# Gated linear attention and a dropless mixture of experts: reordered scan step, work moved between ScalarE and VectorE

## Chip, cores and metric

The kernel runs on one core of one Trainium2 chip. Five engines work side by side, each through its own instructions in order: TensorE (PE, with its weight loads as PEld), VectorE (DVE), ScalarE (ACT), GpSimd (POOL) and SyncE (SP, which here mostly issues DMAs). The metric is the device time of one execution in microseconds (us), less being better. Before the change the median of three runs is 445.88 us (445.43 to 446.48).

## The reference

```python
# attention: B=4, H=8 heads, S=768, D=48
for t in range(S):
    state = alpha[:, :, t, :, None] * state + einsum('bhd,bhe->bhde', k[:, :, t], v[:, :, t])
    y[:, :, t] = einsum('bhd,bhde->bhe', q[:, :, t], state)
x = y.transpose(0, 2, 1, 3).reshape(N, 384)            # N = 3072 tokens
# experts: E=8, F=1024, each token goes to the one with the largest logit
logits = x @ w_gate
expert_idx = argmax(logits, axis=1)
gate_w = softmax(logits)[arange(N), expert_idx]        # 1e-9 added to the sum
for e in range(E):
    h = maximum(x[expert_idx == e] @ w1[e], 0.0)
    y[expert_idx == e] = h @ w2[e]
out = gate_w[:, None] * y
```

No token is dropped, so how many rows an expert gets is known only from the data.

## The kernel before

**The scan.** The sequence is cut into 6 chunks of 128 positions. A tile s = 4c + b is chunk c of batch b with all 8 heads, so there are 24 tiles (NT). Inside a chunk the recurrence is written as a masked product: with cp the running product of alpha and icp its inverse, `operands` makes k*icp and q*cp, `transposes` turns both (kT, qT), `scores` multiplies them per head pair into two PSUM banks sA and sB, `mask` makes dA and dB of them, and `attend` multiplies those with v. What earlier chunks leave comes through the state: `scale_state` scales it (U), `read_state` adds q times U, `keys_values` collects k times v in the same PSUM tile y, and `add_state` adds U and that to the new state (acc). `result` copies y to SBUF (yT), `rows` turns yT into token rows with the gate logits beside them, in PSUM bank x. `logits` adds the logits up (lgn) and takes their minimum (lmin; lgn holds the negated logits), `gate` takes the exponential (gex, its sum is gw), adds 1e-9 and takes the reciprocal, and `keep_rows` scales the rows by it (xs) and stores them in memory. Scaling the rows first is allowed because the gate weight is positive and the expert layers carry no bias.

`logs` takes the logarithm of alpha on ACT (lna), `cums` makes the running sums on PE (bank cum), then icp and cp on ACT, and then issues on ACT's queue one or two small DMAs (L405) that put a row of icp or cp into `dec`, for the decay between chunks: one in the first and in the last chunk with sums, two between. `decay_rows` multiplies these on POOL (er) and `decay_cols` transposes them (ep, then E on DVE), once in a chunk.

**Order.** The scan runs under a manual schedule: the text order of the loop (L656 to L712) is each engine's order. In step i the loop works on several tiles at once: scores, masks and attend of i, result and rows of i-1, logits, gate and keep_rows of i-2, transposes of i+1, operands of i+2, sums and logarithms of up to i+5 tiles. Loads of q, k, v and alpha go through SP two tiles at a time, sums run ahead until tile 23, so that steps from 19 on have none. `route` and the tables before it put the routing work (choice of expert, ranks, slots, one-hot matrices, token lists) into fixed steps. Bank x has one buffer: `rows` of one tile waits until `keep_rows` has read the tile before. At step 23 `early_turn` transposes 256 tokens of expert group 0 that are gathered while the scan still runs, and the tail (L715 to L742) mixes their first layer (`early_layer1`, 8 blocks) with the last rows, choices, ranks, counts and slots.

**The experts.** Group 0's other 168 rows run plainly: `gather` fetches token rows by indirect DMA on POOL, `turn` transposes them (tp on PE, xgT by a copy), `rest_layer1` does 8 blocks of three products with a relu from PSUM on ACT (L1052), `rest_layer2` the second layer. `places`, a Python generator, computes on DVE where each group begins and whether a group overflows; its last part (overflow counts xn, xi, xx) feeds a loop at the end that handles overflowing groups. Groups 1 to 7 run both layers in a Strassen-like form, whose sums of weights are made on DVE by `weight_sums` (s and th, L184 and L187); `layer1` takes a generator `beside` and advances it between its products, so that storing the last group's rows (`rows_out`) and for group 1 the weight sums of layer 2 are spread over it. `weights(i, layer)` reads the expert's number on SP and issues the load of its weights (1.5 MB).

Of the kernel before, what the change touches and what calls it, by code (L numbers as in the profile page):

```python
# [18 lines left out]
def kernel(  # L19
# [343 lines left out]
    with tc.tile_pool(name="ld", bufs=6) as ld, \  # L363
# [65 lines left out]
        def operands(s):  # L429
            d = st[s]  # L430
            kq = kqb[s % 3]
            for i, n, e in ((0, "k", "icp"), (1, "q", "cp")):
                nc.gpsimd.tensor_tensor(  # L433
                    by_half(kq[:, i]), d[n].rearrange("s (a p) d -> s a p d", a=2),
                    d[e][:].rearrange("s (a p d) -> s a p d", a=2, p=NP), op=ALU.mult,
                )

        def transposes(s):
            d = st[s]
            for i, n in enumerate(("kT", "qT")):  # L440
                tp = ps.tile([C, NP, C], F32, name="tp", bufs=2)
                for p in range(NP):
                    nc.tensor.transpose(tp[:, p, :], pair(kqb[s % 3][:, i], p), ident[:])  # L443
                d[n] = work.tile([C, NP, C], F32, name=n)

                if i and s < NT - B - 2:
                    nc.vector.tensor_copy(d[n][:], tp[:])  # L447
                else:
                    nc.scalar.copy(d[n][:], tp[:])
# [74 lines left out]
        def rows(s):  # L524
            d = st[s]
            d["x"] = ps.tile([C, NP, C], F32, name="x")
            for m in range(NP):
                for o in (0, HC):
                    nc.tensor.matmul(  # L529
                        d["x"][o : o + HC, m, : D2 + E], lhsT=d["yT"][:, m // 2, m % 2, o : o + HC], rhs=iw[:, m, :],  # L530
                        start=True, stop=True,
                    )
# [6 lines left out]
        def gate(s):  # L539
            d, t = st[s], s  # L540
            gex = work.tile([C, E], F32, name="gex")
            d["gw"] = work.tile([C, 1], F32, name="gw", bufs=4)
            nc.scalar.activation(gex[:], lgn[:, t, :], AF.Exp, bias=lmin[:, t : t + 1], scale=-1.0, accum_out=d["gw"][:])
            nc.vector.tensor_scalar_add(d["gw"][:], d["gw"][:], 1e-9)
            nc.vector.reciprocal(d["gw"][:], d["gw"][:])
# [91 lines left out]
        def tiles(t0, n):  # L637
# [6 lines left out]
            5 * B: [(one_hots, nc.vector, 11, 12)], 5 * B + 1: [(one_hots, nc.vector, 14, 15)], NT - 1: [(choose, 4)],  # L644
# [11 lines left out]
        for i in range(-4, NT):  # L656
            loads_for(i + 3)
            do(scores, i)
            if i == NT - 1:
                early_turn()  # L660
            do(result, i - 1)
            do(add_state, i - 1)
# [3 lines left out]
            do(mask, i, 1)  # L666
            if -2 < i < 0:
                idle(3)
            do(logits, i - 2)
            do(transposes, i + 1)  # L670
            sums = list(new_sums(i))

            if i < B:
                for s in sums[:1]:
                    cums(s)
            do(gate, i - 2)
            route(i)
            if i == NT - 2:
                si = next(se)[1]
                eg["si"] = lambda j, r: si[:r, j : j + 1]  # L680
            do(keep_rows, i - 2)
            if i >= B:
                for s in sums[:1]:
                    cums(s)
# [10 lines left out]
            do(attend, i)  # L695
            for s in sums[1:]:
                cums(s)
# [8 lines left out]
            for s in new_sums(i + 1):  # L706
                logs(s)
# [8 lines left out]
        result(last)  # L716
        logits(last - 1)
        early_layer1(0)
        rows(last)
        gate(last - 1)  # L720
        keep_rows(last - 1)
        early_layer1(1)
        logits(last)
        choose(NB - 1)
        ranks(NG - 1)
        gate(last)
        keep_rows(last)
        early_layer1(2)
        cps = ps.tile([C, NP, C], F32, name="sA").rearrange("p a c -> p (a c)")[:, : 2 * E]
        counts(NG - 1, cps)  # L730
# [30 lines left out]
    def turn(g):  # L761
        g["xT"] = wk.tile([C, DB, CAP0], F32, name="xgT")
        for j, r in blocks(g):
            tp = mps.tile([C, DB, C], F32, name="tp", tag="tp")
            for a in range(DB):
                nc.tensor.transpose(tp[:, a, :r], g["xg"][:r, j, a * C : (a + 1) * C], ident[:r, :r])  # L766
            nc.vector.tensor_copy(g["xT"][:, :, j * C : j * C + r], tp[:, :, :r])  # L767
# [208 lines left out]
    def places():  # L976
# [26 lines left out]
        nc.vector.tensor_mul(nb[:], nb[:], over[:])  # L1003
        ve = small2("ve")
# [14 lines left out]
        nc.vector.tensor_copy(xi[:], xx[0:1, 0, :])  # L1019

# [5 lines left out]
        yield xn, xi, xx  # L1026
# [14 lines left out]
    def rest_layer1(g):  # L1041
        n = g["n"]
        g["h"] = wk.tile([C, FB, CAP0], F32, name="h_sb")
        for f in range(FB):
# [7 lines left out]
            nc.scalar.activation(g["h"][:, f, :n], hp[:, :n], AF.Relu)  # L1052
# [28 lines left out]
    xn, xi, xx = next(pl)  # L1081
    def beside(i):

        yield from rows_out(groups[i - 1])
        if i == 1:
            for k_, _ in enumerate(weight_sums(groups[1], 2, nc.vector)):
                if k_ % 2:
                    yield

    for i, g in enumerate(groups):  # L1090
# [8 lines left out]
        if i:  # L1099
            layer1(g, beside(i), begin)  # L1100
        else:
            rest_layer1(g)
        weights(i + 2, 1)
        if i == 0:
            weights(1, 2)
        if i + 2 < E:
# [25 lines left out]

    nx = nc.values_load(xn[0:1, 0:1], min_val=0, max_val=NX)
# [47 lines left out]
```

## Time and profile before

| what | value |
| --- | --- |
| median of three runs | 445.88 us |
| the profiled execution, its own time | 446.82 us |
| its span, first to last instruction | 444.7 us |
| PE busy | 411.4 us (93%) |
| PEld busy | 349.2 us (79%) |
| DVE busy | 222.4 us (50%) |
| ACT busy | 170.3 us (38%) |
| POOL busy | 146.9 us (33%) |
| mean granted TensorE clock | 0.987 |
| first `scores` / last `rows` of the scan end | 10.7 / 160.4 us |

The profile is of one execution, 0.94 us above the median of the runs; 2.1 us of its time lie outside the span. Shares are means over the span: the scan (to about 160 us), the early tokens and group 0 (to about 200), and groups 1 to 7 are stages with limits of their own. In rows of the profile, "out<-in" gives the tiles by the program's names, "x" the count, and what stands behind the last bar or in brackets is how long the engine stood idle before the instruction and what ended that wait. ACTq is a DMA issue in ACT's queue. Where T is used, it is the start of a step's first `scores` product; for steps 0, 3, 13, 15, 18, 19 and 23 that is 10.71, 30.42, 92.30, 104.35, 122.47, 127.91 and 150.34 us.

### The profile page before, as it was taken

The page shows a single profiled execution, that of the slowest core. Times are in us where ns is not written, and L with a number is a line of the kernel's source. Part 1 is how long each engine was busy: PE and PEld are TensorE (multiplying, and loading weights), DVE is VectorE, ACT ScalarE, POOL GpSimd, SP SyncE. Part 2 cuts the span into 40 slices and gives each one's busy share as a digit, 9 for nine tenths or more (in the row PEclk, how much of TensorE's full clock was granted, in tenths as well). Part 3 has the DMA queues.
Part 4 walks back from the last instruction along what each step waited for, and adds up shares of the span by engine and source line. Part 5 has one row for each costly group of instructions (what it writes and reads, how often), then busy time and mean ns, then how long its engine had stood idle before and what let it go on. Part 6 is the DMA issues. An engine that isn't in the chain of part 4 may idle for free.

```text
span 444.7 us, 9321 instructions
## 1 busy us (share of the span) xinstructions
PE 411.4 (93%) x3566; PEld 349.2 (79%) x3566; DVE 222.4 (50%) x670; ACT 170.3 (38%) x452; POOL 146.9 (33%) x195
## 2 busy tenths in 40 slices
PE   7898999999998889889899999999999999999991
PEld 5567777877886676679769979979979979979970
DVE  3333645654566546622673474474474473583500
ACT  3565555555654331014412512512513513514411
POOL 3537444677568102700400240230240230201102
PEclk9999999999999999989999999999999999999996
DMA  9999999999540214458233252352353254100101
GB/s 175 202 196 221 214 206 195 241 236 208 124 110 29 68 55 165 124 180 291 60 141 118 79 201 87 110 197 73 124 196 102 94 193 147 46 2 18 33 0 51
DMA packets 119969, 59.07 MB, mean 133 GB/s; under 512 B 102806, under 2 KB 114159, under 8 KB 119924
## 3 DMA queue, kind: packets, MB, share of 16 engines
q1 hardware_dynamic: 114804, 48.80, 42.6%
q0 software_dynamic: 3424, 9.59, 6.3%
q8 instruction: 29, 0.48, 0.5%
q10 hardware_dynamic: 1696, 0.08, 0.2%
q14 instruction: 16, 0.13, 0.1%
HBM read 48.95 MB, written 9.58 MB: 132 GB/s over the span
## 4 chain that ended last, share of the span: by engine, by line
PE 54%; issue 5%; DVE 2%; ACT 1%; POOL 1%; POOLq 0%
PE pA L848 10%; PE pB L848 8%; PE pC L919 7%; PE pA L904 7%; PE pC L848 4%; PE pB L904 4%; PE pA L1036 2%; PE pC L904 2%; PE tp L766 2%; PE pA L1060 2%; PE tp L615 2%; PE pB L1048 1%; PE tp L949 1%; PE pC L1048 1%; DVE xgT L767 1%
## 5 line engine op out<-in xcount | busy, mean ns | idle before, releaser
L936 POOL DMA_INDIRECT out_dram<-zo,sp x25 | 27.2, 1089 | 174.9 <-ACT zo L935 123.6
L792 ACT COPY u<-pA 128x208 f32<-128x208 f32 (+6 forms) x70 | 22.2, 317 | 70.7 <-PE pA L904 67.0
L184 DVE TENSOR_TENSOR h_sb<-pB,u 128x208 f32<-128x208 f32 (+6 forms) x56 | 20.1, 359 | 55.7 <-PE pB L848 40.5
L919 PE MATMUL pC<-h_sb,w 128*128 128x416 f32 (+6 forms) x112 | 38.0, 492 | 0.0
L433 POOL TENSOR_TENSOR kqb<-k_sb,icp 128x384 f32<-128x384 f32 x24 | 24.1, 1002 | 41.8 <-PE y L504 16.4
L919 PEld LDWEIGHTS pC<-h_sb,w 128*128 128x128 f32 x112 | 21.1, 190 | 13.6 <-issue 4.4
L529 PE MATMUL x<-iw,yT 128*64 128x104 f32 x384 | 22.2, 258 | 8.9 <-ACT xs L551 8.8
L756 POOL DMA_INDIRECT xg<-x_rows,gp x25 | 26.7, 1068 | 7.6 <-issue 6.1
L848 PE MATMUL pA<-t,s 128*128 128x208 f32 (+6 forms) x112 | 28.6, 337 | 0.6
L456 PE MATMUL sA<-qT,kT 48*128 48x128 f32 x192 | 27.7, 284 | 0.2 <-DVE qT L447 0.2
L456 PE MATMUL sB<-qT,kT 48*128 48x128 f32 x192 | 27.7, 285 | 0.0
L848 PE MATMUL pA<-xgT,w 128*128 128x208 f32 (+6 forms) x112 | 27.7, 329 | 0.0
L443 PE MATMUL tp<-ident,kqb 128*128 128x128 f32 x192 | 26.4, 279 | 1.1 <-POOL kqb L433 1.1
L529 PEld LDWEIGHTS x<-iw,yT 128*64 128x64 f32 x384 | 17.7, 137 | 11.7 <-ACT xs L551 11.3
L456 PEld LDWEIGHTS sA<-qT,kT 48*128 48x128 f32 x192 | 23.1, 187 | 3.5 <-issue 0.8
L848 PE MATMUL pB<-t,w 128*128 128x208 f32 (+6 forms) x112 | 23.6, 333 | 1.3 <-DVE h_sb L184 0.9
L187 DVE TENSOR_TENSOR th<-h_sb,th 128x208 f32<-128x208 f32 (+6 forms) x56 | 20.2, 360 | 9.2 <-ACT h_sb L861 8.5
L433 POOL TENSOR_TENSOR kqb<-q_sb,cp 128x384 f32<-128x384 f32 x24 | 24.0, 1001 | 1.3 <-DMA q_sb<-in_q_dram 1.3
L522 DVE TENSOR_TENSOR acc<-y,U 128x192 f32<-128x192 f32 x16 | 5.7, 357 | 37.0 <-ACT yT L512 31.0
L443 PEld LDWEIGHTS tp<-ident,kqb 128*128 128x128 f32 x192 | 20.8, 141 | 4.3 <-POOL kqb L433 2.2
L767 DVE COPY xgT<-tp 128x384 f32<-128x384 f32 (+7 forms) x27 | 12.2, 490 | 23.4 <-PE tp L766 23.2
L848 PE MATMUL pC<-xgT,w 128*128 128x208 f32 (+6 forms) x112 | 23.1, 329 | 0.0
(234 smaller groups left out, 975.7 us busy)
## 6 DMA issues: line engine op xcount, KB each, us to landing
w<-in_moe_w_dram SPq DMA_DIRECT2D x14, 1536.0 KB, 6.7
x_rows<-xs SPq DMA_DIRECT2D x24, 192.0 KB, 2.9
a_sb<-in_alpha_dram SPq DMA_DIRECT2D x11, 384.0 KB, 4.4
k_sb<-in_k_dram SPq DMA_DIRECT2D x11, 384.0 KB, 5.8
q_sb<-in_q_dram SPq DMA_DIRECT2D x11, 384.0 KB, 5.6
v_sb<-in_v_dram SPq DMA_DIRECT2D x11, 384.0 KB, 4.8
w<-in_moe_w_dram SPq DMA_DIRECT2D x6, 256.0 KB, 3.6
w<-in_moe_w_dram SPq DMA_DIRECT2D x4, 384.0 KB, 4.4
```

The lines of the kernel that those rows point to most:

```text
L184: eng.tensor_tensor(out, a, b, op=ALU.add)
L187: eng.tensor_tensor(out, a, b, op=ALU.subtract)
L433: nc.gpsimd.tensor_tensor(by_half(kq[:, i]), d[n].rearrange("s (a p) d -> s a p d", a=2), d[e][:].rearrange("s (a p d) -> s a p d", a=2, p ...
L443: nc.tensor.transpose(tp[:, p, :], pair(kqb[s % 3][:, i], p), ident[:])
L456: nc.tensor.matmul(t[:, p, :], lhsT=d["kT"][r : r + D, p, :], rhs=d["qT"][r : r + D, p, :], start=True, stop=True,)
L529: nc.tensor.matmul(d["x"][o : o + HC, m, : D2 + E], lhsT=d["yT"][:, m // 2, m % 2, o : o + HC], rhs=iw[:, m, :], start=True, stop=True,)
L756: nc.gpsimd.indirect_dma_start(out=g["xg"][:r, j, :], out_offset=None, in_=x_d[:, :], in_offset=bass.IndirectOffsetOnAxis(ap=g["gi"](j, r) ...
L792: nc.scalar.copy(t[:, :m], bank["A"][:, :m])
L848: nc.tensor.matmul(out, lhsT=ops[n_][0], rhs=ops[n_][1], start=first and n_ == names[0], stop=True, skip_group_check=True,)
L904: nc.tensor.matmul(out, lhsT=lhs, rhs=rhs, start=first and f == 0, stop=True, skip_group_check=True)
L919: nc.tensor.matmul(d2[:, :n], lhsT=w2[:, f, 2 * C :], rhs=h[:, f, :n], start=(f == 0), stop=(f == FB - 1),)
L936: ins = nc.gpsimd.indirect_dma_start(out=out[:, :], out_offset=bass.IndirectOffsetOnAxis(ap=g["si"](j, r), axis=0), in_=zo[:r], in_offset= ...
```

## The change

It reorders the scan's step and its tail, gives some copies and relus to another engine, and moves one weight load and some DVE work in the first expert groups. What is computed is the same.

1. `operands` of tile 0 runs on DVE, all others stay on POOL. `transposes` copies kT of tiles 0 to 2 on DVE (it was ACT).
2. `rows` of the last tile writes bank sA; the last `counts` takes bank x instead.
3. `gate` keeps the exponential; the addition and reciprocal become `gate_weight`. In the step, result, logits, gate and the logarithms (which stood at the end of the step before) come right behind scores; add_state stands behind logits for i >= 4 and behind the masks for i < 4 (it stood behind result); `cums` stands ahead of gate_weight and keep_rows in every step (for i >= 4 it stood behind keep_rows). On ACT a step's order is thus yT, gex, lna, kT, icp, cp, the `dec` DMAs, xs; before it was yT, kT, gex, xs, icp, cp, the DMAs, lna. PE's order of operations stays.
4. result(22), which result's first place in step 23 would have held, comes at the end of step 22, early_turn in step 23 behind logits, gate and logs. choose(4) moves a step earlier. The tail is reordered.
5. `turn` copies odd blocks on ACT. `rest_layer1` does odd relus on DVE, and behind each a piece of `places`, which now yields between pieces.
6. `beside` for group 1 takes one step of storing and one weight sum at a call in turn; before, the sums came behind all the storing, two at a call.
7. The load of w2 for group 1 is issued right behind that of w1 for group 1, ahead of w1 for group 2, and in SP's order ahead of the read of xn.

```diff
@@ -429,8 +429,9 @@
         def operands(s):
             d = st[s]
             kq = kqb[s % 3]
+            eng = nc.gpsimd if s else nc.vector
             for i, n, e in ((0, "k", "icp"), (1, "q", "cp")):
-                nc.gpsimd.tensor_tensor(
+                eng.tensor_tensor(
                     by_half(kq[:, i]), d[n].rearrange("s (a p) d -> s a p d", a=2),
                     d[e][:].rearrange("s (a p d) -> s a p d", a=2, p=NP), op=ALU.mult,
                 )
@@ -443,7 +444,7 @@
                     nc.tensor.transpose(tp[:, p, :], pair(kqb[s % 3][:, i], p), ident[:])
                 d[n] = work.tile([C, NP, C], F32, name=n)
 
-                if i and s < NT - B - 2:
+                if s < B - 1 or i and s < NT - B - 2:
                     nc.vector.tensor_copy(d[n][:], tp[:])
                 else:
                     nc.scalar.copy(d[n][:], tp[:])
@@ -523,7 +524,8 @@
 
         def rows(s):
             d = st[s]
-            d["x"] = ps.tile([C, NP, C], F32, name="x")
+
+            d["x"] = ps.tile([C, NP, C], F32, name="x" if s < NT - 1 else "sA")
             for m in range(NP):
                 for o in (0, HC):
                     nc.tensor.matmul(
@@ -541,6 +543,9 @@
             gex = work.tile([C, E], F32, name="gex")
             d["gw"] = work.tile([C, 1], F32, name="gw", bufs=4)
             nc.scalar.activation(gex[:], lgn[:, t, :], AF.Exp, bias=lmin[:, t : t + 1], scale=-1.0, accum_out=d["gw"][:])
+
+        def gate_weight(s):
+            d = st[s]
             nc.vector.tensor_scalar_add(d["gw"][:], d["gw"][:], 1e-9)
             nc.vector.reciprocal(d["gw"][:], d["gw"][:])
 
@@ -641,7 +646,7 @@
             B + 1: [(choose, 0)], 2 * B + 1: [(choose, 1)], 2 * B + 2: [(ranks, 0)],
             2 * B + 3: [(slots, 0, 2 * B + 1)], 3 * B: [(rows_cols, 0)], 3 * B + 1: [(choose, 2)],
             4 * B + 1: [(choose, 3), (ranks, 1)], 4 * B + 2: [(slots, 1, 4 * B)], 4 * B + 3: [(rows_cols, 1)],
-            5 * B: [(one_hots, nc.vector, 11, 12)], 5 * B + 1: [(one_hots, nc.vector, 14, 15)], NT - 1: [(choose, 4)],
+            5 * B: [(one_hots, nc.vector, 11, 12)], 5 * B + 1: [(one_hots, nc.vector, 14, 15)], NT - 2: [(choose, 4)],
         }
         on_gpsimd = {3 * B + 1: tiles(0, 3), 3 * B + 2: tiles(3, 3), 4 * B: tiles(6, 2), 5 * B: tiles(8, 3), 5 * B + 1: (13,)}
         counts_in = {2 * B + 2: 0, 4 * B + 1: 1}
@@ -656,32 +661,35 @@
         for i in range(-4, NT):
             loads_for(i + 3)
             do(scores, i)
+            if i < NT - 1:
+                do(result, i - 1)
+            do(logits, i - 2)
+            if i >= B:
+                do(add_state, i - 1)
+            do(gate, i - 2)
+            if i > 0:
+                for s in new_sums(i):
+                    logs(s)
             if i == NT - 1:
                 early_turn()
-            do(result, i - 1)
-            do(add_state, i - 1)
             if 0 < i < NT and i % B == 0:
                 decay_cols(i // B)
             do(mask, i, 0)
             do(mask, i, 1)
+            if i < B:
+                do(add_state, i - 1)
             if -2 < i < 0:
                 idle(3)
-            do(logits, i - 2)
             do(transposes, i + 1)
             sums = list(new_sums(i))
-
-            if i < B:
-                for s in sums[:1]:
-                    cums(s)
-            do(gate, i - 2)
+            for s in sums[:1]:
+                cums(s)
+            do(gate_weight, i - 2)
             route(i)
+            do(keep_rows, i - 2)
             if i == NT - 2:
                 si = next(se)[1]
                 eg["si"] = lambda j, r: si[:r, j : j + 1]
-            do(keep_rows, i - 2)
-            if i >= B:
-                for s in sums[:1]:
-                    cums(s)
             do(operands, i + 2)
             if i < NT - 2:
                 do(scale_state, i)
@@ -693,6 +701,8 @@
                     scale_state(s)
             do(read_state, i)
             do(attend, i)
+            if i == NT - 2:
+                result(i)
             for s in sums[1:]:
                 cums(s)
             do(keys_values, i)
@@ -703,8 +713,9 @@
             do(rows, i - 1)
             if i in counts_in:
                 counts(counts_in[i], counted(i - 1))
-            for s in new_sums(i + 1):
-                logs(s)
+            if i < 0:
+                for s in new_sums(i + 1):
+                    logs(s)
             if i == -3:
                 second_consts()
             late_consts(i - 1)
@@ -714,20 +725,22 @@
 
         last = NT - 1
         result(last)
+        early_layer1(0)
         logits(last - 1)
-        early_layer1(0)
         rows(last)
         gate(last - 1)
-        keep_rows(last - 1)
         early_layer1(1)
         logits(last)
+        gate(last)
+        gate_weight(last - 1)
+        keep_rows(last - 1)
         choose(NB - 1)
         ranks(NG - 1)
-        gate(last)
+        early_layer1(2)
+        cps = ps.tile([C, NP, C], F32, name="x").rearrange("p a c -> p (a c)")[:, : 2 * E]
+        counts(NG - 1, cps)
+        gate_weight(last)
         keep_rows(last)
-        early_layer1(2)
-        cps = ps.tile([C, NP, C], F32, name="sA").rearrange("p a c -> p (a c)")[:, : 2 * E]
-        counts(NG - 1, cps)
         slots(NG - 1, cps)
         rows_cols(NG - 1)
         for f in range(3, FB):
@@ -764,7 +777,7 @@
             tp = mps.tile([C, DB, C], F32, name="tp", tag="tp")
             for a in range(DB):
                 nc.tensor.transpose(tp[:, a, :r], g["xg"][:r, j, a * C : (a + 1) * C], ident[:r, :r])
-            nc.vector.tensor_copy(g["xT"][:, :, j * C : j * C + r], tp[:, :, :r])
+            (nc.scalar.copy if j % 2 else nc.vector.tensor_copy)(g["xT"][:, :, j * C : j * C + r], tp[:, :, :r])
 
     def row_sums(g):
         m = g["n"] // 2
@@ -1001,6 +1014,7 @@
         nb = small2("nb")
         nc.vector.reduce_sum(nb[:], og[:], axis=AX)
         nc.vector.tensor_mul(nb[:], nb[:], over[:])
+        yield
         ve = small2("ve")
         nc.vector.tensor_tensor_scan(ve[:], nb[:], zero_e[:], 0.0, op0=ALU.add, op1=ALU.add)
         xn = small2("xn", (1, 1), I32)
@@ -1017,13 +1031,15 @@
         nc.vector.tensor_scalar_min(xx[:, 0, :], xx[:, 0, :], float(E - 1))
         xi = small2("xi", (1, NX), I32)
         nc.vector.tensor_copy(xi[:], xx[0:1, 0, :])
+        yield
 
         nc.vector.tensor_sub(xb[:], xb[:], xa[:])
         nc.vector.scalar_tensor_tensor(vb[:], in0=first[:], scalar=1.0 / C, in1=vb[:], op0=ALU.mult, op1=ALU.subtract)
         nc.vector.tensor_tensor(xb[:], xb[:], vb[:, None, :].to_broadcast([C, NX, E]), op=ALU.mult)
         nc.vector.reduce_sum(xx[:, 1, :], xb[:], axis=AX)
         nc.vector.scalar_tensor_tensor(xx[:, 1, :], in0=xx[:, 1, :], scalar=2.0, in1=kx[:], op0=ALU.add, op1=ALU.add)
-        yield xn, xi, xx
+        pd.update(xn=xn, xi=xi, xx=xx)
+        yield
 
     def cols_of(t, c0):
         return lambda j, r: t[:r, c0 + j : c0 + j + 1]
@@ -1038,7 +1054,7 @@
                 start=(f == 0), stop=(f == FB - 1),
             )
 
-    def rest_layer1(g):
+    def rest_layer1(g, beside):
         n = g["n"]
         g["h"] = wk.tile([C, FB, CAP0], F32, name="h_sb")
         for f in range(FB):
@@ -1049,7 +1065,11 @@
                     hp[:, :n], lhsT=g["w1"][:, a, f * C : (f + 1) * C], rhs=g["xT"][:, a, :n],
                     start=(a == 0), stop=(a == DB - 1),
                 )
-            nc.scalar.activation(g["h"][:, f, :n], hp[:, :n], AF.Relu)
+            if f % 2:
+                nc.vector.tensor_scalar_max(g["h"][:, f, :n], hp[:, :n], 0.0)
+                next(beside, None)
+            else:
+                nc.scalar.activation(g["h"][:, f, :n], hp[:, :n], AF.Relu)
 
     def rest_layer2(g, d):
         n = g["n"]
@@ -1078,14 +1098,12 @@
     turn(g0)
     early_layer2(1, 1)
     scatter(eg, 1, C, eg["z"][:, :Dm])
-    xn, xi, xx = next(pl)
     def beside(i):
 
-        yield from rows_out(groups[i - 1])
-        if i == 1:
-            for k_, _ in enumerate(weight_sums(groups[1], 2, nc.vector)):
-                if k_ % 2:
-                    yield
+        work = [rows_out(groups[i - 1])] + [weight_sums(groups[1], 2, nc.vector)] * (i == 1)
+        while work:
+            work = [w for w in work if next(w, w) is not w]
+            yield
 
     for i, g in enumerate(groups):
         nxt = groups[i + 1] if i + 1 < E else None
@@ -1099,10 +1117,10 @@
         if i:
             layer1(g, beside(i), begin)
         else:
-            rest_layer1(g)
-        weights(i + 2, 1)
+            rest_layer1(g, pl)
         if i == 0:
             weights(1, 2)
+        weights(i + 2, 1)
         if i + 2 < E:
             gather(groups[i + 2])
 
@@ -1130,6 +1148,7 @@
         pass
     in_order.close()
 
+    xn, xi, xx = pd["xn"], pd["xi"], pd["xx"]
     nx = nc.values_load(xn[0:1, 0:1], min_val=0, max_val=NX)
     with tc.If(nx > 0):
         with tc.For_i(0, nx, 1) as i:
```

## The prediction

> **What bounds it now.** I read the page first: TensorE against the other engines, then the group with most idle time ahead of it.
>
> ```profile
> PE   7898999999998889889899999999999999999991
> PEclk9999999999999999989999999999999999999996
> L529 PE MATMUL x<-iw,yT 128*64 128x104 f32 x384 | 22.2, 258 | 8.9 <-ACT xs L551 8.8
> ```
>
> TensorE bounds the kernel (411.4 of 444.7 us), at an almost full clock (mean 0.987): only its idle time, 33.3 us, can go. The page puts the scan's share on one operation: `rows` (L529) waits for `xs` (L551). The view by windows, cut at the first `scores` matmul of steps 3, 15, 23 and at the second-last `rows`, places it:
>
> ```profile
> 0.00:30.42 30.42, 26.10 (x239) 18.08 (x239) 10.79 (x26) 15.90 (x34) 12.99 (x26) 1.00 1.00 194
> 30.42:104.35 73.93, 69.19 (x1083) 55.85 (x1081) 40.19 (x122) 39.82 (x96) 44.47 (x75) 1.00 1.01 215
> 104.35:150.34 45.99, 43.20 (x694) 35.56 (x693) 26.98 (x94) 24.24 (x58) 29.31 (x40) 1.00 0.46 109
> 150.34:160.40 10.06, 6.77 (x95) 5.42 (x93) 3.22 (x14) 4.04 (x11) 0.00 (x0) 1.00 0.11 42
> 182.30:193.70 11.40, 8.76 (x49) 7.99 (x48) 4.29 (x12) 2.33 (x8) 6.12 (x6) 0.88 0.35 101
> ```
>
> Second column length, third PE busy, last but two the clock, then the DMA share. Idle: 4.3, 4.7, 2.8, 3.3 us in the scan, 2.6 in group 0's layer 1. DMA is saturated until step 15.
>
> An unstalled step is the sum of its PE rows (step 18, 122.47 to 127.91): 5.44 us; `rows` starts T+4.61, T being the step's first `scores`. Every fourth step adds 0.49 (end-of-chunk transposes). Step 13 (T = 92.30), timeline of ACT, DVE, PE:
>
> ```profile
> 93.43 0.57 ACT L512 COPY yT<-y 128x512 f32<-128x512 f32 x1
> 94.10 0.36 DVE L522 TENSOR_TENSOR acc<-y,U 128x192 f32<-128x192 f32 x1 [2.48 <-ACT yT L512]
> 95.98 0.30 ACT L543 ACTIVATE gex<-lgn,lmin 128x8 f32<-128x8 f32 x1 [1.31 <-DVE lmin L537]
> 96.83 0.58 ACT L551 ACTIVATE xs<-x,gw 128x384 f32<-128x384 f32 x1 [0.46 <-DVE gw L545]
> 97.47 0.94 PE L529 MATMUL x<-iw,yT 128*64 128x104 f32 x16 [0.39 <-ACT xs L551]
> ```
>
> The chain is yT, acc, masks, lmin, gex, gw, xs (T+4.53), rows (T+5.17, 0.56 late).
>
> **The scan steps.** The new order puts logits before masks and gex before everything but yT: gw is then ready near T+2.5, and that chain no longer decides. But cums now precede keep_rows everywhere, so on ACT icp, cp and both `dec` DMA issues stand ahead of xs. Before has one step of that order, step 3 (T = 30.42):
>
> ```profile
> 33.35 0.49 ACT L396 ACTIVATE icp<-cum 128x384 f32<-128x384 f32 x1 [0.56 <-PE cum L393]
> 33.87 0.50 ACTq L405 DMA_DIRECT2D dec<-icp  x1
> 34.47 0.55 ACTq L405 DMA_DIRECT2D dec<-cp  x1
> 35.06 0.30 ACT L543 ACTIVATE gex<-lgn,lmin 128x8 f32<-128x8 f32 x1 [0.84 <-DVE qT L447]
> ```
>
> The instruction behind the second issue starts at T+4.64. PE's own order does not change, so cum comes no earlier, and xs takes that place: end T+5.22, rows T+5.28 (0.06 later, as in step 13), step 5.28 + 0.86 = 6.14; with chunk-end transposes 6.58.
> - Steps 3 to 14: 9 x 6.14 + 3 x 6.58 = 75.0, and 0.54 for the count products of step 10: 75.5 against 73.93: **+1.6**. The old wait is replaced by its twin. The ends: if ACT finds room to run xs before the issues, all twelve stalls of 0.67 go (-6.4 in place of +1.6); if the issues last as they did, +2.
> - Steps 15 to 18 issue one `dec`: the gap from cp to the next ACT instruction is 0.69 there (109.95 to 110.64) against 1.32 to 1.35, so xs ends before T+4.61. 5.46, 5.91 (chunk end), 6.0 (counts), 5.46 = 22.8 against 23.56: **-0.7**.
> - Steps 19 to 22 have no cum (5.44 - 0.74 = 4.70), from 20 on no L504 either (4.35). Step 20 adds chunk-end transposes and a late U, step 21 one-hot products of 1.0; waits of 0.65 and 0.58 for xs go: 4.70, 5.6, 5.5, 4.42 = 20.2 against 22.43, of which I count **-2.1**.
>
> [...] In step 20 the DVE copy of E (L283) at 131.70 took 2.82 us, where its like takes 0.17, while POOL ran three products back to back (131.59 to 134.49). [...] by the row it loses all three. I take 0.6 of it gone; the ends are -1.2 and +0.5.
>
> **Start.** First operands on DVE: two products of 128x384 with SBUF inputs, about 0.55 each (128x512 took 0.68, 128x208 0.37) against POOL's 1.00: -0.96 at step 0. But step 2's and step 4's products wait for inputs at 15.53, 17.04, 26.48, 28.31:
>
> ```profile
> POOL kqb L433 <- DMA k_sb<-in_k_dram: 8.3, 2, 5.9
> ```
>
> With the DMA share at 1.00 this gain is lost at step 2's transposes. What returns is the masks ahead of add_state and both early kT copies on DVE: 0.78, 0.26, 0.46 of PE waits for dA and rows up to step 3, and 0.1 of the first step. **-1.6** (-0.3 to -2.0).
>
> **Step 23** (T = 150.34):
>
> ```profile
> 152.35 0.86 ACT L609 COPY k_sb<-tp 128x384 f32<-128x384 f32 x2 [2.92 <-PE tp L608]
> 153.09 0.60 ACT L512 COPY yT<-y 128x512 f32<-128x512 f32 x1
> 153.84 0.66 PE L483 MATMUL y<-qT,U 48*48 48x128 f32 x16 [1.49 <-ACT yT L512]
> 159.51 0.93 PE L529 MATMUL x<-iw,yT 128*64 128x104 f32 x16 [1.80 <-ACT xs L551]
> ```
>
> The early token copies stand ahead of yT; with result(22) a step earlier that wait of 1.49 goes. The last rows wait 1.80 for xs to leave bank x; in sA they wait for nothing. **-3.3**; first rows of the tail then wait for yT alone (0.6 on ACT). From 160.4 to 170.4 PE is busy 9.95 of 10.00, and DVE's slot chain ends 1.5 us early: the gain passes through, the reordered exponentials and counts being beside PE work.
>
> **Group 0, weights.** L1048 by line, 182 to 194:
>
> ```profile
> L1048 PE MATMUL pB<-xgT,w 128*128 128x168 f32 x24 | 5.2, 362 | 0.9 <-ACT h_sb L1052 0.9
> L1048 PE MATMUL pC<-xgT,w 128*128 128x168 f32 x24 | 4.6, 335 | 1.7 <-ACT h_sb L1052 1.7
> ```
>
> Relus on two engines can save at most these 2.6 and some lateness around them (eight blocks at 0.855 would end near 189.3, not 193.7: -4.4). But ACT was free: it began each relu when PE's block ended (187.27, 190.07 where 184.0 was due), and why PE's blocks end late no view shows; the clock there is 0.88. So no gain is the near end; I take **-1.0** (0 to -4.4).
>
> w2(1) is issued right behind w1(1) instead of behind the xn wait. Gather g0 (issued 172.23) landed at 177.80, as w1's load ended, against 1.3 to 2.1 with no weight load. [...] by that row the gather waits for the queue to drain, 3.9 us more (1.5 MB at 400 GB/s). The packets near 262 decide: the gather's pass among a weight load's that runs on. [...] **+0.7** (0 to +4).
>
> **Group 1.** In its layer 1 DVE's weight sums (L184, L187, 0.68 each) ran ahead of h_sb; PE idles 0.47 at 217.6 and 0.85 at 222.07. One sum per call and an earlier w2: **-1.1** (0 to -1.4). **Turns:** second copies on ACT; PE waits 2.3 at L766 over 7 times, mostly for the first block, which stays on DVE: **-0.3** (0 to -0.6). Places in pieces only move DVE work of 4.1 us behind relus; if uncovered they would hold the turn of group 1 by up to 1, in the range. All else (205.96 of 209.00 busy in 224 to 433) stands.
>
> **Sum.** -1.6 + 1.6 - 0.7 - 2.1 - 3.3 + 0.7 - 1.0 - 1.1 - 0.3 = -7.8. The profiled execution took 446.82 (span 444.7 and 2.1 around it): 439.0. It lies 0.94 above the median 445.88, so the forecast is **438.1**.
>
> **Rivals.**
> - A, xs not in the way: the ACT triggers shrink or the relu split frees PE. For: step 13's chain really shortens. Against: step 3's row. Twelve steps x 0.67 = -8.0 would give 430; half of it, or the full -4.4, 434. Chance 0.17.
> - B, only the end gains: start and middle are DMA-bound (share 1.00), so 3.0 of the start and of steps 15 to 22 is lost, or the gather drains behind w2: about 442. For: DMA rows. Against: steps 19 to 23 have share 0.11 to 0.5. Chance 0.25.
> - C, slower: the `dec` issues ahead of xs take longer once they meet input loads queued at share 1.01. Each extra us stands once in each of 12 steps; from 7.8/12 = 0.65 us more per step the change loses, at 1.0 more it takes 450. Against: every issue in the trace took 0.50 to 0.55. Chance 0.05.
> - D, nothing of it reaches the end, because the stall only moves to the gather: 445.9. Chance 0.03.
>
> **Numbers.** Forecast 0.50 (436.5 to 440.5). The range 432.5 to 442.5 takes in most of A and B and the ends of relu and gather. The measurement tells 0.2% (0.9 us) from none: faster 0.92, same 0.03, slower 0.05.
>
> **Signs.** Right: rows still wait about 0.67 for xs in steps 3 to 14, ACT showing two `dec` issues just ahead; no wait at L529 from step 15; last rows end 6 us earlier. Wrong: xs before T+4.4 in the middle (A), g0 landing over 2 us later after its issue (B), issues over 1 us (C).

## The result, and the profile after

The changed kernel takes 438.97 us in the median of four runs (438.96 to 439.68) against 445.65 (443.92 to 446.48) before: a ratio of 0.9859, 95% interval 0.9828 to 0.989. Its profiled execution took 438.98, with a span of 436.9 against 444.7. The forecast was 438.1 (for a profiled execution 439.0). The total was hit, but two of its terms were wrong, by +2.4 and -3.6 us, and covered each other. The page of the changed kernel, with the lines that answer those shown of before (L531 here is L529 there):

```profile
PE   8798998889999999999999999999999999999991
PEclk9999999999999999999999999999999999999996
L531 PE MATMUL x<-iw,yT 128*64 128x104 f32 x368 | 21.4, 258 | 7.8 <-ACT xs L556 7.7
```

`rows` still waits for `xs`: 7.8 us instead of 8.9. The page alone says that little happened there. The view by windows, cut at the same events, says where it moved (length, then PE busy; the last three numbers are the clock, the DMA share and GB/s):

```profile
0.00:29.68 29.68, 25.46 (x238) 17.90 (x238) 13.62 (x31) 14.31 (x31) 10.74 (x24) 1.00 1.01 193
29.68:107.60 77.92, 69.25 (x1082) 55.99 (x1080) 36.90 (x122) 40.34 (x97) 44.78 (x75) 1.00 0.96 208
107.60:130.80 23.20, 23.20 (x370) 19.13 (x368) 11.76 (x42) 14.71 (x34) 13.16 (x18) 1.00 0.66 139
130.80:151.16 20.36, 19.36 (x326) 16.48 (x324) 13.75 (x54) 10.23 (x24) 16.06 (x23) 1.00 0.29 80
151.16:157.84 6.68, 6.68 (x94) 5.36 (x92) 2.49 (x11) 3.09 (x10) 0.00 (x0) 1.00 0.16 60
180.56:187.40 6.84, 6.84 (x50) 6.84 (x48) 4.37 (x20) 1.72 (x5) 5.13 (x6) 1.00 0.53 161
```

The middle of the scan (second row) grew from 73.93 to 77.92 us while its PE work stayed at 69.2: PE idles 8.7 us there, against 4.7. From step 15 to the last rows PE is busy for 49.2 of 50.2 us. Group 0's relu blocks (last row) have no gap.

| stage | before | after | difference | forecast |
| --- | --- | --- | --- | --- |
| to the first scores of step 3 | 30.42 | 29.68 | -0.74 | -1.6 |
| steps 3 to 14 | 73.93 | 77.92 | +3.99 | +1.6 |
| steps 15 to 18 | 23.56 | 23.20 | -0.36 | -0.7 |
| steps 19 to 22 | 22.43 | 20.36 | -2.07 | -2.1 |
| step 23, to the end of the last rows | 10.04 | 6.68 | -3.36 | -3.3 |
| tail, early layer 2, to the turn of group 0 | 18.47 | 18.72 | +0.25 | 0 |
| turn of group 0 to its first relu block | 3.41 | 4.00 | +0.59 | +0.7 |
| relu blocks of group 0 | 11.46 | 6.84 | -4.62 | -1.0 |
| rest of group 0 | 9.19 | 9.02 | -0.17 | 0 |
| group 1, to its long layer-2 products | 21.64 | 20.31 | -1.33 | -1.1 |
| from there to the end | 220.15 | 220.17 | +0.02 | -0.3 |
| span | 444.70 | 436.90 | -7.80 | -7.8 |

Two rows need explaining: why the middle lost 4.0 us, and whether the split relus really gained 4.6.

### The profile page after: what moved, and what is told of

The parts are those of the page before. It is cut to its first block, busy times and chain, and to the rows that moved or that the text cites. A ratio compares the mean times of both kernels' runs of the same rounds, so it can differ in the third digit from the quotient of the medians.

```text
span 436.9 us, 9317 instructions
## 1 busy us (share of the span) xinstructions
PE 408.0 (93%) x3566; PEld 347.5 (80%) x3566; DVE 217.0 (50%) x667; ACT 172.5 (39%) x457; POOL 144.0 (33%) x193
## 4 chain that ended last, share of the span: by engine, by line
PE 71%; issue 7%; DMA 6%; ACT 4%; POOL 4%; DVE 3%; ACTq 2%; SPq 0%; POOLq 0%
PE pA L861 10%; PE pB L861 8%; PE pC L932 7%; PE pA L917 7%; PE pC L861 4%; PE sA L457 4%; PE x L531 4%; PE pB L917 4%; PE tp L444 4%; PE cum L393 3%; PE pC L917 2%; PE y L494 2%; ACTq L405 2%; DMA x_rows<-xs 2%; PE tp L779 2%
## 5 line engine op out<-in xcount | busy, mean ns | idle before, releaser
L434 POOL TENSOR_TENSOR kqb<-k_sb,icp 128x384 f32<-128x384 f32 x23 | 23.0, 1001 | 52.3 <-PE y L505 18.9
L538 DVE TENSOR_REDUCE lgn<-x 128x8 f32<-128x32 f32 x23 | 4.4, 192 | 51.3 <-PE x L531 45.6
L531 PE MATMUL x<-iw,yT 128*64 128x104 f32 x368 | 21.4, 258 | 7.8 <-ACT xs L556 7.7
L531 PEld LDWEIGHTS x<-iw,yT 128*64 128x64 f32 x368 | 16.9, 136 | 9.8 <-ACT xs L556 9.4
L434 POOL TENSOR_TENSOR kqb<-q_sb,cp 128x384 f32<-128x384 f32 x23 | 23.0, 999 | 1.8 <-DMA q_sb<-in_q_dram 1.8
L457 PEld LDWEIGHTS sB<-qT,kT 48*128 48x128 f32 x192 | 23.1, 187 | 0.0
```

What stands on the lines that cost most here:

```text
L434: eng.tensor_tensor(by_half(kq[:, i]), d[n].rearrange("s (a p) d -> s a p d", a=2), d[e][:].rearrange("s (a p d) -> s a p d", a=2, p=NP), ...
L457: nc.tensor.matmul(t[:, p, :], lhsT=d["kT"][r : r + D, p, :], rhs=d["qT"][r : r + D, p, :], start=True, stop=True,)
L531: nc.tensor.matmul(d["x"][o : o + HC, m, : D2 + E], lhsT=d["yT"][:, m // 2, m % 2, o : o + HC], rhs=iw[:, m, :], start=True, stop=True,)
```

## The experiments

Theory for the middle (Q): ACT issues two small DMAs ahead of xs, and each delay of that queue falls on PE. Its rival (L): the stretch is bound by its loads (DMA share 0.96 to 1.01), and rows only shows the wait. For the relus: the split frees PE (S), or the long stretch of before was an accident of one execution (R).

**1. The kernel before, profiled again** (no edit).

> The kernel before, profiled a second time. In its first profile the eight relu blocks of group 0 (L1048, from the first block to the second layer) took 11.46 us, of which 3.4 us at half clock, against 6.84 in the changed kernel. If the relus on one engine are the cause (S), the stretch takes 11 to 12 us again. If it was an accident of that execution (R), it takes 7 to 9 us here and the span is 2 to 4 us shorter than 444.7. The scan's milestones should repeat within 0.3 us either way.

444.63 us, span 442.5. Its windows, step 23 to the last rows and then the relu blocks of group 0:

```profile
151.45:163.10 11.65, 8.31 (x94) 6.84 (x92) 3.22 (x14) 4.05 (x11) 0.00 (x0) 0.85 0.09 34
184.98:191.82 6.84, 6.84 (x49) 6.83 (x48) 4.35 (x13) 2.66 (x8) 5.24 (x5) 1.00 0.44 127
```

With relus on ACT alone the blocks take 6.84 us, as in the changed kernel: R. The half clock, which lay in group 0 in the first profile, lies in step 23 here (0.85 in the clock column, PE busy 8.31 us for work that took 6.77). The span was 2.2 us shorter, as R had it. The milestones did not all repeat within 0.3: step 3 to step 15 took 74.61 instead of 73.93, with one `dec` issue of 1.63 us in it. Against this profile the changed kernel is 5.6 us shorter, with nothing from the relus.

**2. All relus on ACT.**

```diff
-            if f % 2:
-                nc.vector.tensor_scalar_max(g["h"][:, f, :n], hp[:, :n], 0.0)
-                next(beside, None)
-            else:
-                nc.scalar.activation(g["h"][:, f, :n], hp[:, :n], AF.Relu)
+            nc.scalar.activation(g["h"][:, f, :n], hp[:, :n], AF.Relu)
+            if f % 2:
+                next(beside, None)
```

> The changed kernel with all eight relus of group 0 on ACT again, the placing arithmetic still drawn in pieces. S: the stretch goes from 6.84 back to about 11 us and the time rises by 4 us (to 443). R: one ACT relu takes 0.31 us against 0.86 us of products, so nothing waits; the stretch stays near 6.9 and the time within 0.5 us of 439.0.

437.58 us (ratio to before 0.9849, interval 0.9811 to 0.9887). The blocks take 6.84 us again. The split relus bring nothing; S falls. The time is 1.4 us below the changed kernel's, more than the 0.5 that R allowed. That this is the relus' doing is not shown: in the profiles 0.5 lies in steps 0 to 14, and 0.5 between the turn and the first block, where executions of the same order differ by as much (77.4 to 77.9 in steps 3 to 14, and 3.47 to 4.00 at the turn).

**3. cums behind keep_rows again, the early gate kept.**

```diff
+            if i < B:
+                for s in sums[:1]:
+                    cums(s)
-            for s in sums[:1]:
-                cums(s)
             do(gate_weight, i - 2)
             route(i)
             do(keep_rows, i - 2)
+            if i >= B:
+                for s in sums[:1]:
+                    cums(s)
```

> The changed kernel with cums behind keep_rows again for steps 4 and up, the early gate kept. Theory Q (the two dec DMA issues ahead of xs on ACT hold up the rows): all waits of rows for xs in steps 4 to 14 go (6.6 us of the 7.7 at L531), the middle (first scores of step 3 to that of 15) falls from 77.9 to about 71, the kernel to about 432. Rival L (the middle is bound by loads, the DMA share being 0.96 to 1.01): the wait moves to products of operands on POOL or to transposes, the middle stays above 75 and the kernel above 436.5.

429.88 us, ratio 0.9677 (0.964 to 0.9714). Steps 3 to 14 take 68.48 us: 9.4 less than in the changed kernel and 5.4 less than before.

```profile
28.73:97.21 68.48, 66.99 (x1082) 55.10 (x1081) 37.25 (x122) 38.66 (x96) 44.40 (x74) 1.00 1.04 225
```

L falls: the loads are the same, and the stretch is shorter. They now move at 225 GB/s, against 208 in the changed kernel and 215 before, so the DMA share of about 1, which the prediction read as "saturated", was no limit in these steps.

**4. Only the `dec` issues behind keep_rows**, icp and cp where the change put them.

```diff
             st[s]["cp"], st[s]["icp"] = cp, icp
+        def dec_rows(s):
+            c, b = cb(s)
+            cp, icp = st[s]["cp"], st[s]["icp"]
             for cc, i, row in ...:                      # the L405 DMAs
...
             do(keep_rows, i - 2)
+            for s in sums[:1]:
+                dec_rows(s)
...
             for s in sums[1:]:
                 cums(s)
+                dec_rows(s)
```

> The changed kernel with cums where the change put it, but its dec DMA issues moved behind keep_rows: only these issues change places with xs. Q: xs starts right behind cp, near T+3.9, the waits of rows for xs go, the middle falls to about 71 and the kernel to about 432, as with cums late. L: middle above 75, kernel above 436.5. If only cums late gains, it is icp and cp, not the issues, that hold xs up.

428.81 us, ratio 0.9676 (0.962 to 0.9733). One step of each on ACT and PE shows it. First the changed kernel, timeline of step 13 (T = 95.27):

```profile
98.20 0.49 ACT L396 ACTIVATE icp<-cum 128x384 f32<-128x384 f32 x1 [0.56 <-PE cum L393]
99.32 0.55 ACTq L405 DMA_DIRECT2D dec<-cp  x1
99.91 0.58 ACT L556 ACTIVATE xs<-x,gw 128x384 f32<-128x384 f32 x1 [0.84 <-DVE sel L248]
100.54 0.94 PE L531 MATMUL x<-iw,yT 128*64 128x104 f32 x16 [0.49 <-ACT xs L556]
```

xs starts at T+4.64 in this step, to the hundredth where the forecast had it; in most others it is T+4.69 or 4.70. The releaser in the brackets (sel) is not the cause: xs needs x and gw, gw was ready at T+3.34 (the forecast had T+2.5), and the issue just above ends at 99.87. Now the same order with the issues behind, step 14 (T = 91.67):

```profile
94.60 0.49 ACT L396 ACTIVATE icp<-cum 128x384 f32<-128x384 f32 x1 [0.56 <-PE cum L393]
95.12 0.50 ACTq L407 DMA_DIRECT2D dec<-icp  x1
95.36 0.59 ACT L558 ACTIVATE xs<-x,gw 128x384 f32<-128x384 f32 x1
95.72 0.55 ACTq L407 DMA_DIRECT2D dec<-cp  x1
96.29 0.90 PE L533 MATMUL x<-iw,yT 128*64 128x104 f32 x16
```

icp stands at the same place in the step (T+2.93), xs at T+3.69, rows at T+4.62 without a wait. The first issue stands behind xs in ACT's order and is yet shown ahead of it, at 95.12: it took 95.12 to 95.62, xs 95.36 to 95.95. In these rows an issue holds up what stands behind it in the text, not what stands ahead. The step is 5.45 us long instead of 6.19. The longest of PE's waits over the scan, first in the changed kernel (us, times, longest):

```profile
PE x L531 <- ACT xs L556: 7.7, 11, 1.6
```

With the issues behind keep_rows this wait is gone from the list, and the next one leads it:

```profile
PE y L486 <- POOL U L474: 2.3, 2, 1.3
```

Steps 3 to 14 take 68.64 us. This is the run that shows the cause: only the issues changed places.

**5. The end of the scan alone, on the kernel before.**

```diff
-            d["x"] = ps.tile([C, NP, C], F32, name="x")
+            d["x"] = ps.tile([C, NP, C], F32, name="x" if s < NT - 1 else "sA")
...
-            do(result, i - 1)
+            if i < NT - 1:
+                do(result, i - 1)
...
             do(attend, i)
+            if i == NT - 2:
+                result(i)
...
-        cps = ps.tile([C, NP, C], F32, name="sA").rearrange(...)
+        cps = ps.tile([C, NP, C], F32, name="x").rearrange(...)
```

> The kernel before with the end of the scan alone changed: last rows in bank sA, counts in x, the copy of tile 22 a step earlier. Theory E: both waits of step 23 go (1.49 and 1.80), from the first scores of step 23 to the last rows it takes 6.7 us instead of 9.9, the gain of 3.3 reaches the end, and with the sparse stretch gone the half-clock window that the kernel before shows in about half of its runs (mean clock 0.987 to 0.989 against 0.992 to 0.994) no longer opens there: a clock of 0.992 or more in all runs, and 4 to 5 us less in the median (about 440). Rival F: the half-clock window has nothing to do with step 23: mean clocks stay mixed, and the median falls by 3.3 or less.

440.8 us in the median of nine against 444.48 of fourteen; ratio 0.9933 (0.9906 to 0.996). The turn of group 0 comes at 176.33 instead of 178.85: the 2.5 us won in step 23 are still there. The 3.3 is not reached. Neither of the two old waits is left, but the first rows of the tail now wait for xs:

```profile
154.64 0.94 PE L529 MATMUL x<-iw,yT 128*64 128x104 f32 x16 [0.80 <-ACT xs L551]
```

In the changed kernel, where the gate comes early, this wait is gone (PE busy for 6.68 of 6.68 us). Two of the nine runs have a mean clock of 0.987 and 0.989; of the fourteen of before beside them, seven are at 0.989 or below. E holds for the waits, and for the clock only in part: the median fell by 3.7, between the two forecasts, and one run at 0.993 took 443.32, so the clock is not all that varies.

**6. Group 1's weight sums as before**, and **7. the weight loads as before.**

```diff
-        work = [rows_out(groups[i - 1])] + [weight_sums(groups[1], 2, nc.vector)] * (i == 1)
-        while work:
-            work = [w for w in work if next(w, w) is not w]
-            yield
+        yield from rows_out(groups[i - 1])
+        if i == 1:
+            for k_, _ in enumerate(weight_sums(groups[1], 2, nc.vector)):
+                if k_ % 2:
+                    yield
```

> The changed kernel with group 1's second-layer weight sums behind the storing and two at a call again. If the sums ahead of DVE's h_sb adds were the cost, group 1 from its first product to the long second-layer products takes 21.1 us again against 19.9. If the earlier w2 load was what helped, it stays near 19.9.

```diff
-        if i == 0:
-            weights(1, 2)
         weights(i + 2, 1)
+        if i == 0:
+            weights(1, 2)
```

> The changed kernel with w2 of group 1 issued behind w1 of group 2 again. If w2 behind w1 holds up the gather of group 0, the time from the first block's turn to the first relu block falls from 4.0 to 3.4 us and DMA xg no longer ends a PE wait there. Group 1 stays at 19.9 if the spread sums alone made its gain, and is longer if the early load did.

The kernels took 439.65 and 439.26 us, one run each, and are read by their profiles. Group 1, cut as in the table, takes 21.64 us with the old sums and 20.30 with the old loads, against 20.31 in the changed kernel: the spread sums are worth 1.3, the early load nothing. With the old loads, turn to first block takes 3.42 instead of 4.00. This row of the changed kernel's PE timeline (the second block of the turn) shows the wait that the early load brings:

```profile
177.57 0.38 PE L779 MATMUL tp<-ident,xg 40*128 40x40 f32 x3 [0.46 <-DMA xg<-x_rows,agi]
```

The two gathers of group 0 landed 6.6 and 6.4 us after their issue instead of 5.9 and 5.0. The cost varies: all seven profiles with the old order of loads have 3.41 or 3.42 in this row of the table, the seven with the new one 3.47 to 4.00.

**8. Tile 0 on POOL, early kT on ACT again.**

```diff
-            eng = nc.gpsimd if s else nc.vector
+            eng = nc.gpsimd
...
-                if s < B - 1 or i and s < NT - B - 2:
+                if i and s < NT - B - 2:
```

> The changed kernel with tile 0's operands on POOL and the first kT copies on ACT again. If the start is bound by loads, the first scores come 1.0 us later and step 3 starts within 0.4 us of 29.7; if the DVE operands make the start's gain, step 3 starts about 1 us later (30.7).

437.86 us in one run. The first scores come at 10.40 instead of 9.35, and step 3 starts at 29.12 instead of 29.68. The microsecond won at the first scores is not seen at step 3. That the loads decide there is argued, not shown; and single executions scatter: five profiles with the same text up to step 3 reach it at 28.73 to 30.17.

**9, 10. All three found wanting taken out, with the relus split and on ACT.** The edits are those of 4, 7 and 8, for the second also that of 2.

> The changed kernel without the three parts that the runs so far show to cost or to bring nothing: dec issues behind keep_rows, the old order of the weight loads, tile 0 on POOL and ACT. From 428.8 for the dec issues alone: 0.6 less where the gather no longer waits behind w2, and 0 to 0.8 for the start: 427.5 to 428.3, and no wait of 0.3 us or more of rows for xs in steps 5 to 23.

> The same with all relus of group 0 on ACT. If the split relus are worth nothing, within 0.6 us of the kernel with the split; if DVE's relus and placing pieces get in the way of group 1's turn, 0.5 to 1.5 us faster; if they free PE, slower by as much.

434.86 us (0.9641, 0.9613 to 0.9669) and 432.42 us (0.9589, 0.956 to 0.9618). These runs were on a chip on which the kernel before took 451.08, so only the ratios can be compared with other runs. Both profiles show group 0 lengthened again, with a half-clock stretch, here with all relus on ACT:

```profile
170.12:183.08 12.96, 8.68 (x49) 8.16 (x48) 4.16 (x12) 2.33 (x8) 5.95 (x6) 0.90 0.29 88
```

Neither gave the 427.5 to 428.3 expected. The kernel with all relus on ACT was 2.4 us faster than its twin with the split, more than the 0.5 to 1.5 named for relus on DVE that get in the way; as in experiment 2 the split is the slower of the two, and where the time goes is open. The lengthening had by then been seen in three kernels with the old order of loads and in none with the new. The next pair asks whether that order is its cause (W).

**11, 12. A pair that differs in the order of the loads alone** (10 again, and 10 without the edit of 7).

> The dec issues behind keep_rows, tile 0 on POOL and ACT, all relus of group 0 on ACT, and w2 of group 1 issued right behind w1 as the change has it. In the profiles so far group 0's relu blocks were lengthened (8.6 to 13.0 us instead of 6.84) only in kernels with the old order of the loads (3 of 6), never with the new (0 of 6). Theory W: the new order prevents it; the blocks take 6.84 us and this kernel is 1.5 us or more faster than its pair. Rival: it is chance or the chip; both kernels show it alike and lie within 0.8 us, this one 0.5 later by the gather.

> Its pair: the same with w2 of group 1 behind w1 of group 2 (the same text as best_act). W: group 0's relu blocks lengthened in the profile or a half-clock window in most runs (mean clock 0.990 or less), and 1.5 us or more slower than pair_early. Rival: within 0.8 us of it.

428.39 us (0.9631, 0.96 to 0.9662) and 428.15 us (0.9625, 0.9592 to 0.9657), with 6.84 us for the relu blocks in both. W finds no support: with the old order, too, there is no lengthening here. But the text that took 432.42 on one chip takes 428.15 on this other one, so that the order matters on the first is not excluded. Both beat the changed kernel and the one before; so does experiment 4 with its single edit, and by their intervals the three cannot be told apart.

## Why the prediction was right, and where it was not

**The middle: right mechanism, a term too small.** The step said that xs would take the place behind two issues at T+4.64 and rows stall about 0.67. The trace shows T+4.64 to 4.70 and waits of 0.49 to 0.57 in most steps, a step of 6.19 against the 6.14 forecast. What was mis-sized is "9 x 6.14 + 3 x 6.58 = 75.0", by 2.4 us: the nine plain steps took 0.6 more together, and the three with chunk-end transposes 7.16, 6.66 and 7.68 instead of 6.58. Step 4 first:

```profile
40.45 1.07 ACTq L405 DMA_DIRECT2D dec<-cp  x1
41.62 0.58 ACT L556 ACTIVATE xs<-x,gw 128x384 f32<-128x384 f32 x1 [1.42 <-issue]
```

Its second issue took 1.07, so that xs came at T+5.66. Here PE also waited 0.94 for U, which POOL made only after two products of operands, at 39.60; the two delays ended together. But in two profiles of the same order (experiments 7 and 8) PE has no such wait in step 4, and the step is no shorter (7.27 and 7.78, with issues of 1.19 and 1.70). In all five profiles of this order that issue takes 1.07 to 1.70 us. Then step 12, the steepest one:

```profile
92.37 1.30 ACTq L405 DMA_DIRECT2D dec<-cp  x1
93.77 0.58 ACT L556 ACTIVATE xs<-x,gw 128x384 f32<-128x384 f32 x1 [1.67 <-issue]
94.41 0.93 PE L531 MATMUL x<-iw,yT 128*64 128x104 f32 x16 [1.60 <-ACT xs L556]
```

Of an issue of 1.30, 0.75 more than usual, PE waits all of it; the other 0.3 of this step came before icp, which stood at T+3.65 instead of 3.37. So the forecast's price of 0.50 to 0.55 for every issue was the mis-sized term, and rival C, at a chance of 0.05, was right in part. The line against C, "every issue in the trace took 0.50 to 0.55", was a misreading: the first profile has one of 0.78 at 104.44, and the step behind it took 6.25 instead of 6.02. Why an issue is long is not shown.

So +1.6 became +4.0 (+3.3 to +4.0 over the five profiles of this order), and experiments 3 and 4 show what it stands for: the rest of the reordering is worth -5.3 to -5.4 in this stretch, and the issues in front of xs take 9.3 to 9.4 back. The near end that the forecast had named ("all twelve stalls go", -6.4 in place of +1.6) is nearly what another order of the lines brings.

**Steps 15 to 18: half.** xs does not end before T+4.61, as the forecast had it, but at T+4.63, and rows start at T+4.69 instead of 4.62: each step is 0.1 longer than with the issue behind xs, and -0.7 became -0.4.

**Group 0's relus: wrong.** "I take -1.0 (0 to -4.4)" rested on the first profile's stretch of 11.46. The bound of 0 was the right answer: relus on ACT alone take 6.84 us as well. The 4.6 us of the table are what that one execution of before happened to lose. The step had noted that ACT waited for PE, not PE for a busy ACT, and that no view gave a reason; a stall with no cause in the profile should have been left out of the sum until a second profile showed it.

**The forecast total was therefore lucky.** Its own sign "last rows end 6 us earlier" did not come: they end 2.5 us earlier (157.84 against 160.38). The missing 3.5 us came back in group 0, where that one execution of before had lost 4.6. Without the relu term the two profiles differ by -3.2 us, yet the medians of the runs by -6.7. A part of the gap may be the half clock: by its mean clock (0.984 to 0.989 against 0.990 and more) the kernel before has it in about half of its runs on two of the chips. In the last set of its runs those at 0.991 or more took 443.04 to 444.64, those at 0.984 to 0.989 took 443.6 to 447.03; all four runs of the changed kernel are at 0.991 to 0.993. But one half-clock stretch of 3.41 us costs, as an estimate, at most half its length, 1.7 us, and not every run has one; the rest of the gap stays open. The removed waits of step 23 may be what keeps the clock up (experiment 5); that was not shown.

**Step 23, gather, group 1: right** within 0.3 us each, and by the named causes: experiment 5 for the last rows' bank and the early copy, 7 for the gather, 6 for the sums. The +0.7 for the gather was the author's estimate; the +0.6 of the table is the dear end of what it cost (0.1 to 0.6), and its delay of 0.7 to 1.4 us is well short of the 3.9 worked out for a queue that drains first. The early w2, which the forecast gave part of group 1's gain, brings none. **Steps 19 to 22: right in the sum alone** (-2.1): step 20 took 5.0 instead of 5.6 and step 21 6.15 instead of 5.5. The wait for U had moved to step 21, where PE waited 1.00 for it, behind POOL's one-hot products and operands.

**Start: half.** The DVE operands were given nothing ("this gain is lost at step 2's transposes"), and -1.6 for masks and kT copies was -0.74. Step 3 starts at 30.22 to 30.70 in three profiles of the old start and at 28.73 to 30.17 in five of the new one, so about 0.8 us seems real. Putting the DVE operands and kT copies back did not cost it in experiment 8 (29.12); with the issues behind xs the one profile with the new start has 28.48 and four with the old operands and copies 29.34 to 30.01, so a share of theirs is not excluded.

**The long DVE row.** The instruction at 131.70 in before is the cast L283, in step 19 (the prediction called it the copy of E, which is L427 and stood behind it in step 20). In the changed kernel's DVE timeline the same cast reads:

```profile
133.74 0.98 DVE L283 CAST ti<-tr 128x8 int32<-128x8 f32 x1
```

POOL's product beside it began at 133.68 and took 1.01, and POOL paused 0.39 us behind it: here the cast took as long as one product, against the 0.17 of its like. In three profiles of the old order, where POOL's products follow each other without a pause, a DVE instruction at this place took 2.77 to 2.85 us, as long as three products. Why it took so long is not shown, and no run changes the pause alone.

**Turns: wrong by 0.3.** The stretch from group 1's long products to the end did not change (220.15 and 220.17): the second copies on ACT bring nothing there.

## To carry to other kernels

When a compute instruction on ACT is the last thing before the bound engine, look at the DMA issues that the program text puts ahead of it in the same queue: here two issues of half a microsecond and the longer ones among them took back 9.3 us where the reordering had brought 5.3, and moving them behind one line freed it. A stage that is long in one profile, with no cause in any view, needs a second profile before its length goes into a sum. And a wait on PE may cost more than its length, if the granted clock falls behind it, as in the rows below (0.50 for 3.41 us, behind 3.41 us of which PE was busy for 1.88); that was seen, not tested alone.

## What the runs showed that was not expected

**Where the half clock stood.** In the first profile the record of the granted clock begins at 6.65 us and changes at 190.97, 194.38 and 436.73, which is 54, 1 and 71 times 3.413 us further each time; in that of the changed kernel it begins at 5.46 and changes at 428.71, 124 times 3.413 us later. The clock was 0.50 from 190.97 to 194.38, in group 0. In the second profile of before a half-clock stretch of the same length lies in step 23 (second row; the first is the stretch of 3.41 us ahead of it):

```profile
151.69:155.10 3.41, 1.88 (x27) 1.55 (x29) 1.55 (x4) 1.64 (x5) 0.00 (x0) 1.00 0.08 30
155.10:158.51 3.41, 3.41 (x44) 3.03 (x41) 1.00 (x6) 1.15 (x2) 0.00 (x0) 0.50 0.16 58
```

In the first row PE was busy for 1.88 of 3.41 us, 55%. Ahead of the other half-clock stretches inside a kernel it was busy for 48% (first profile of before, 1.63 of 3.42 us), 48% (experiment 9, 1.62 of 3.40) and 13% (experiment 10, 0.43 of 3.40). Stretches no fuller were also followed by full clock: in the first profile PE was busy for 49% of 33.95 to 37.37 and for 47% of 156.83 to 160.25, and the clock was 1.00 in the 3.41 us behind each. So these rows do not show what brings the half clock. The price, as an estimate, is at most half of the 3.41 us, 1.7; in step 23 PE was busy 1.5 us longer (8.31 against 6.77). That is about as much again as PE's idle time in the first row (1.53; the wait for yT in step 23 of the first profile was 1.49).

**Relus that start late.** In the first profile of before and in experiments 9 and 10, relus of group 0's first layer start up to 3 us and more after the profile shows PE done with their block. In experiment 10, PE began the second block at 170.98 and needs 0.86 for one, but:

```profile
175.29 0.31 ACT L1073 ACTIVATE h_sb<-pB 128x168 f32<-128x168 f32 x1 [3.80 <-PE pC L1069]
```

Three of fourteen profiles show it, two of them on one chip. It is not the relus' engine (9 and 10 both have it). It is not the old order of the loads alone: four of the seven profiles with that order are free of it, though all seven with the new order are. Whether PE's word came late or PE's rows are shown early the profile does not tell; the cause is open.
